# Splitting a V product stream between the sums of the next pair in a decode attention kernel

## The chip, the cores and the metric

The kernel runs on one core of a Trainium2 chip. The metric is device time in microseconds (us); before the change the median of three runs is 1988.61 us. A core has four engines that compute (TensorE for matmuls, VectorE, ScalarE, GpSimd), each with an instruction stream of its own, and SyncE, whose stream issues the large loads here. The streams meet only at semaphores. In the profile the engines are PE (and PEld for its weight loads), DVE, ACT, POOL and SP.

## The reference

Two independent attention blocks, A and B, each decode one token for two sequences, and their outputs are put side by side:

```python
def _A_ref(x, k_cache, v_cache, wq, wo):          # B = 2, Sq = 1, D = 640
    q = (x @ wq).reshape(B, Sq, Hq, Dh).transpose(0, 2, 1, 3)     # 32 heads of 192
    scores = jnp.einsum("bhqd,bhkd->bhqk", q, k) * (Dh ** -0.5)   # 8192 keys
    p = _softmax(scores, axis=-1)
    o = jnp.einsum("bhqk,bhkd->bhqd", p, v)
    return o.transpose(0, 2, 1, 3).reshape(B, Sq, Hq * Dh) @ wo
```

Everything is in bfloat16. Each block reads a K and a V cache of 2 x 32 x 8192 x 192 elements, each element once: 805 MB, and 837 MB with the weights.

## The kernel before

**Pairs.** The work is cut into 64 pairs (`NP`), each of two heads of one sequence. A pair's K is 6.3 MB, and so is its V. Both lie on 128 partitions: 64 partitions hold one head, and each holds 128 positions (`T`) of 192 elements.

**The ring of loads.** K and V go through three buffers of 6.3 MB (`ring`), in the order K0, V0, K1, V1 and so on; for the last two pairs it is K62, K63, V62, V63. SP issues them in that order (L134), each when its buffer is free: a K buffer when VectorE's fourth product of that K is done (`("m", i, 3)`), a V buffer when the last of its products on TensorE is done (`("pv", i)`). With three buffers, K of pair i+1 goes into the buffer of V of pair i-1, and V of pair i+1 into that of K of pair i. Since SP takes its stream in order, V's issue stands behind K's.

**A pair's scores.** The dot products of a one-row query are made in four quarters. VectorE multiplies a quarter of K by the query, which has been copied to all partitions (`add_mul`, L233; two product buffers `prod`). TensorE adds up the 192 elements in twelve steps of 16 with an identity matrix, into a PSUM tile of 32 x 16 (`add_sum`, L238; two tiles `scps`). VectorE reduces the last 16 (`add_red`, L245). The third product needs the buffer of sum 0, and the fourth that of sum 1. When four quarters are there, VectorE takes the maximum (`add_max`, L250 and L251), POOL takes it over the partitions (L254), and ScalarE makes exp in two halves with its sums (`add_exp`, L259 to L266), into `pb`.

**A pair's output.** `add_pv` has TensorE make one small matmul for the softmax sums (L274) and then 64 matmuls of `pb` with V (`T // 2`, L281), that add up in one PSUM tile (`ops`, two of them). Then ScalarE copies the odd head's part (`add_od`, L292), VectorE makes a reciprocal, an addition and a scaling (`add_on`, L296, L298, L300), and TensorE puts the result with four small matmuls in its place in a collecting tile (`add_place`, L310).

**The order.** Each engine's order is the order in which the main loop adds its operations to that engine's stream. For pair i TensorE runs: sum 0, sum 1, sum 2, the placing of pair i-1, the query of pair i+2 (L218), sum 3, the softmax sums and all 64 products of pair i. VectorE runs: products 0 and 1, the three small operations of pair i-1, reduction 0, product 2, reduction 1, product 3, reductions 2 and 3, the maximum. The last two pairs' products come after the loop, so that pair 63's sums run ahead of pair 62's products.

**Ahead and behind.** Before the loop the two query projections run from loads of 2 x 7.9 MB; behind it the output weights (2 x 7.9 MB, into the same ring) are multiplied with the collected outputs.

Of the kernel before, what the change touches and what calls it, by code (L numbers as in the profile page):

```python
# [51 lines left out]
def build_kernel(nc, blocks, out):  # L52
    NBLK = len(blocks)
    B, Hn, Sk, Dh = blocks[0]["k"].shape
# [4 lines left out]
    NP = NBLK * B * PB  # L59
    LAST = NP - 1  # L60
    T = 128
# [14 lines left out]
    def pair(i):  # L76
        blk, r = divmod(i, B * PB)
        b, ii = divmod(r, PB)
        return blk, b, ii

    with ExitStack() as es:
# [4 lines left out]
        ring = [sb(f"ring{i}", [128, RW], BF16) for i in range(3)]  # L86
# [4 lines left out]
        pb = [sb(f"pb{i}", [128, T // 2, 34], BF16) for i in range(2)]  # L91
# [18 lines left out]
        ops = [ps(f"ops{i}", [128, 512], F32) for i in range(2)]  # L110
# [6 lines left out]
        S_pe = _Stream("pe", sem("s_pe"), reg)  # L117
# [22 lines left out]
        slot_of = {}  # L140
# [6 lines left out]
        for blk in range(NBLK):  # L147
            w = blocks[blk]["wq"].rearrange("(j c) n -> j (c n)", c=DC)
# [23 lines left out]
        for blk, pieces in ((0, WA), (1, WB)):  # L172
            w = blocks[blk]["wo"].rearrange("(p r) n -> p (r n)", r=WR)
# [16 lines left out]
        def pr3(qd):  # L190
            return prod[qd % 2][:].rearrange("p (t d) -> p t d", d=Dh)

        def key(name, i, *rest):
            return (name, i) + rest if i >= 0 else None

        def before(i, qd, n):
            k = 4 * i + qd - n
            return (k // 4, k % 4) if k >= 0 else None
# [16 lines left out]
        def add_q(i):  # L215
            blk, b, ii = pair(i)
            r0 = 32 * blk
            S_pe.add(lambda eng: eng.matmul(qps[:, 0:2 * Dh], selb[r0:r0 + 2, b, :],  # L218
                                            qrow[r0:r0 + 2, 2 * ii * Dh:(2 * ii + 2) * Dh], start=True, stop=True),
                     waits=[("qe", blk, NQC - 1), ("init",), key("qt", i - 1)], sig=("q", i))  # L220

        def add_qt(i):
            def fn(eng):
                eng.activation(qt[i % 3][0:64, :], qps[0:64, 0:Dh], ACTF.Identity)  # L224
                return eng.activation(qt[i % 3][64:128, :], qps[64:128, Dh:2 * Dh], ACTF.Identity)  # L225
            S_act.add(fn, waits=[("q", i), key("m", i - 3, 3)], sig=("qt", i))

        def add_mul(i, qd):
            q = qt[i % 3][:].unsqueeze(1).broadcast_to([128, TQ, Dh])
            prev = before(i, qd, 2)  # L230
            w = [("k", i), ("qt", i)]
            w += [("s",) + prev] if prev else [("pr", 0, NQC - 1), ("pr", 1, NQC - 1)]
            S_dve.add(lambda eng: eng.tensor_tensor(pr3(qd), quarter(i, qd), q, ALU.mult), waits=w, sig=("m", i, qd))  # L233

        def add_sum(i, qd):
            def fn(eng):
                for j in range(NJ):
                    ins = eng.matmul(scps[qd % 2][:], ident[:], pr3(qd)[:, :, j * DG:(j + 1) * DG],  # L238
                                     start=(j == 0), stop=(j == NJ - 1))
                return ins  # L240
            prev = before(i, qd, 2)
            S_pe.add(fn, waits=[("m", i, qd), ("init",), ("r",) + prev if prev else None], sig=("s", i, qd))

        def add_red(i, qd):
            S_dve.add(lambda eng: eng.tensor_reduce(sc[i % 2][:, qd * TQ:(qd + 1) * TQ], scps[qd % 2][:], AXL.X, ALU.add),  # L245
                      waits=[("s", i, qd), key("exp", i - 2)], sig=("r", i, qd))

        def add_max(i):
            def fn(eng):
                eng.tensor_reduce(mp[i % 2][0:64, 0:1], sc[i % 2][0:64, :], AXL.X, ALU.max)  # L250
                return eng.tensor_reduce(mp[i % 2][64:128, 1:2], sc[i % 2][64:128, :], AXL.X, ALU.max)  # L251
            S_dve.add(fn, waits=[("r", i, 0), ("r", i, 1), ("r", i, 2), ("r", i, 3), key("ar", i - 2), ("init",)],
                      sig=("mx", i))
            S_pool.add(lambda eng: eng.partition_all_reduce(mg[i % 2][:], mp[i % 2][:], 128, bass.bass_isa.ReduceOp.max),  # L254
                       waits=[("mx", i), key("nb", i - 2)], sig=("ar", i))
# [14 lines left out]
                return ins  # L270
            S_act.add(fn, waits=[("nb", i), ("r", i, 3), key("pv", i - 2), key("l", i - 2), ("init",)], sig=("exp", i))

        def add_pv(i):
            S_pe.add(lambda eng: eng.matmul(ops[i % 2][0:2, 448:449], rs[i % 2][:], ones[:], start=True, stop=True),  # L274
                     waits=[("exp", i), key("on", i - 2), ("qe", 1, NQC - 1), ("init",)], sig=("l", i))
            vv = ring[slot_of["v", i]][:].rearrange("p (j f) -> p j f", f=2 * Dh)

            def part(j0, j1):
                def fn(eng):
                    for j in range(j0, j1):  # L280
                        ins = eng.matmul(ops[i % 2][0:34, 0:2 * Dh], pb[i % 2][:, j, :], vv[:, j, :],  # L281
                                         start=(j == 0), stop=(j == T // 2 - 1))
                    return ins
                return fn
            if i == LAST:
                S_pe.add(part(0, T // 4), waits=[("exp", i), ("v", i)])
                S_pe.add(part(T // 4, T // 2), waits=[("v2", i)], sig=("pv", i))
            else:
                S_pe.add(part(0, T // 2), waits=[("exp", i), ("v", i)], sig=("pv", i))

        def add_od(i):
            S_act.add(lambda eng: eng.activation(oodd[i % 2][:], ops[i % 2][32:34, Dh:2 * Dh], ACTF.Identity),  # L292
                      waits=[("pv", i), key("on", i - 2)], sig=("od", i))

        def add_on(i):
            S_dve.add(lambda eng: eng.reciprocal(rc[i % 2][:], ops[i % 2][0:2, 448:449]),  # L296
                      waits=[("l", i), ("pv", i), key("on", i - 2)], sig=("rc", i))
            S_dve.add(lambda eng: eng.tensor_tensor(oodd[i % 2][:], ops[i % 2][0:2, 0:Dh], oodd[i % 2][:], ALU.add),  # L298
                      waits=[("od", i)], sig=("ad", i))
            S_dve.add(lambda eng: eng.tensor_scalar(on[i % 2][:], oodd[i % 2][:], rc[i % 2][:], None, ALU.mult),  # L300
                      waits=[("rc", i), ("ad", i), key("pl", i - 2)], sig=("on", i))

        def add_place(i):
            blk, b, ii = pair(i)
            sec = (blk * B + b) * WR

            def fn(eng):
                for a in range(4):
                    at = 128 - (8 * ii + a)
                    ins = eng.matmul(oall[:, sec:sec + WR], place[:, at:at + 128], on[i % 2][:, a * WR:(a + 1) * WR],  # L310
                                     start=(ii == 0 and a == 0), stop=(ii == PB - 1 and a == 3))
                return ins
            w = [("on", i), ("init",)]
            if ii == 0 and i > 0:
                w.append(("oa", i // PB - 1))
            S_pe.add(fn, waits=w, sig=("pl", i))
            if ii == PB - 1:
                S_act.add(lambda eng: eng.activation(oallS[blk][:, :, b], oall[:, sec:sec + WR], ACTF.Identity),
                          waits=[("pl", i)], sig=("oa", i // PB))
# [43 lines left out]
        def fn_x(eng):  # L363
            for c in range(DC):
# [4 lines left out]
                  waits=[("xp",)], sig=("xT",))  # L369
        for blk in range(NBLK):  # L370
            for n in range(NQC):
                add_proj(blk, n)
            if blk == 0:
                for i in range(2):
                    add_q(i)
                    add_qt(i)

        for i in range(NP):
            tail = i >= NP - 2
            add_mul(i, 0)  # L380
            add_mul(i, 1)
            add_sum(i, 0)
            if i and i < LAST:
                add_od(i - 1)
                add_on(i - 1)
            add_red(i, 0)
            add_mul(i, 2)
            add_sum(i, 1)
            add_red(i, 1)
            add_mul(i, 3)  # L390
            add_sum(i, 2)
            if i and i < LAST:
                add_place(i - 1)
            add_red(i, 2)
            if i + 2 < NP:
                add_q(i + 2)
                add_qt(i + 2)
            add_sum(i, 3)
            add_red(i, 3)
            add_max(i)  # L400
            add_exp(i)
            if not tail:
                add_pv(i)
        for i in (NP - 2, NP - 1):
            add_pv(i)
            add_od(i)
            add_on(i)
            if i == NP - 2:
                add_place(i)
# [77 lines left out]
```

## Time and profile before

| what | us |
|---|---|
| median of three runs | 1988.61 (1987.79 to 1988.74) |
| profiled execution, its time | 1987.13 |
| profiled execution, its span | 1985.3 |
| VectorE's products, 256 of | 3.352 each, 852.7 in all |
| TensorE's products with V, 4096 of | 809.4 busy in all |
| TensorE's sums, 3072 matmuls | 700.1 busy in all |
| first product of VectorE starts | 56.67 |
| last K is issued | 1891.96 |

The span runs from the first instruction to the last of the slowest core, and is a little shorter than the time. A matmul's recorded length is longer than its distance to the next, since matmuls overlap; so a stream's length is read from the start of its first to the start of what follows. A group that is "idle before" an instruction names what ended the wait. Where a line of the timeline has an entry "x64", it merges that many instructions.

TensorE's clock is granted in stretches of 3.41 us; over the span it was 0.917 of full speed on average, alternating between full and half.

### The profile page before, as it was taken

To read this page: it belongs to the slowest core of one execution; us is meant where nothing else is said; L and a number is where in the kernel's file an instruction comes from. 1 tells how busy PE (TensorE), PEld (TensorE's weight loads), DVE (VectorE), ACT (ScalarE), POOL (GpSimd) and SP (SyncE) were. 2 spreads that over 40 slices of the span, in tenths; PEclk is the share of its full clock that TensorE was granted. 3 is DMA by queue.
4 is the path that set the end of the run, shared out by engine and by line. 5 is a ranking of instruction groups with operands and counts; after the bars stand their busy time and mean duration, and the time that the engine had idled before them with its cause. 6 is when DMAs were issued, how large, how long until landed. Compare 5 with 4: busy or idle time off the path is not lost.

```text
span 1985.3 us, 17767 instructions
## 1 busy us (share of the span) xinstructions
PE 1578.6 (80%) x7933; PEld 762.0 (38%) x7933; DVE 1095.1 (55%) x833; ACT 186.9 (9%) x610; POOL 32.2 (2%) x82
## 2 busy tenths in 40 slices
PE   4777877877877877877877877877877877878878
PEld 1333433433433433433433433433433433433434
DVE  0655655655555655655555565555555555565561
ACT  2111001011011011011011010010010010010000
POOL 1000000000000000000000000000000000000000
PEclk9989989989899989989889899889989889899889
DMA  9999999999999999999999999999999999999999
GB/s 412 437 428 430 439 427 427 426 424 415 413 430 429 410 431 410 432 427 421 416 424 426 419 425 418 420 429 418 421 418 426 421 424 419 423 424 420 415 428 380
DMA packets 20836, 837.91 MB, mean 422 GB/s; under 512 B 2316, under 2 KB 2584, under 8 KB 2968
## 3 DMA queue, kind: packets, MB, share of 16 engines
q1 hardware_dynamic: 20744, 836.78, 99.1%
q8 instruction: 62, 1.02, 0.2%
q14 instruction: 14, 0.11, 0.0%
q10 hardware_dynamic: 16, 0.01, 0.0%
HBM read 836.77 MB, written 0.01 MB: 421 GB/s over the span
## 4 chain that ended last, share of the span: by engine, by line
issue 91%; PE 4%; DMA 3%; DVE 2%; POOL 1%; SPq 0%; ACT 0%; POOLq 0%; DVEq 0%
DMA prod<-in_B_wq_dram 2%; PE ops L281 2%; DVE prod L233 1%; POOL mg L254 1%; PE scps L238 1%; PE ops L205 1%; DMA ring<-in_B_wo_dram 1%; DVE sc L245 0%; SPq L134 0%; ACT pb L266 0%; POOLq L43 0%; DVE mp L251 0%; ACT out_sb L333 0%; PE ops L274 0%; DVE oodd L298 0%
## 5 line engine op out<-in xcount | busy, mean ns | idle before, releaser
L233 DVE TENSOR_TENSOR prod<-ring,qt 128x6144 bf16<-128x6144 bf16 x256 | 852.7, 3352 | 388.2 <-DMA ring<-in_A_k_cache_dram 183.0
L238 PE MATMUL scps<-prod,ident 128*128 128x512 bf16 x3072 | 700.1, 381 | 152.6 <-DVE prod L233 152.6
L281 PE MATMUL ops<-ring,pb 128*34 128x384 bf16 x4096 | 809.4, 367 | 0.0
L281 PEld LDWEIGHTS ops<-ring,pb 128*34 128x34 bf16 x4096 | 440.3, 109 | 346.4 <-issue 138.2
L238 PEld LDWEIGHTS scps<-prod,ident 128*128 128x128 bf16 x3072 | 285.7, 98 | 538.7 <-DVE prod L233 198.9
L245 DVE TENSOR_REDUCE sc<-scps 128x32 f32<-128x512 f32 x256 | 176.1, 688 | 247.3 <-PE scps L238 247.3
L274 PE MATMUL ops<-ones,rs 128*2 128x1 f32 x128 | 12.2, 164 | 224.0 <-ACT pb L266 224.0
L296 DVE RECIPROCAL rc<-ops 2x1 f32<-2x1 f32 x64 | 10.0, 156 | 219.5 <-PE ops L281 219.5
L274 PEld LDWEIGHTS ops<-ones,rs 128*2 128x2 f32 x128 | 5.5, 82 | 255.1 <-ACT pb L266 254.6
L292 ACT ACTIVATE oodd<-ops 2x192 f32<-2x192 f32 x64 | 20.6, 321 | 820.3 <-PE ops L281 820.3
L266 ACT ACTIVATE pb<-sc,nb 64x128 bf16<-64x128 f32 x128 | 81.4, 636 | 3.1
L224 ACT ACTIVATE qt<-qps 64x192 bf16<-64x192 f32 x64 | 20.7, 323 | 566.7 <-PE qps L218 566.7
L254 POOL PARTITION_ALL_REDUCE mg<-mp x64 | 25.8, 404 | 1903.7 <-DVE mp L251 1903.7
L259 ACT ACTIVATE nb<-mg 64x1 f32<-64x1 f32 x64 | 13.0, 203 | 323.2 <-POOL mg L254 323.2
L266 ACT ACTIVATION_READ_ACCUMULATOR pb<-sc,nb 64x1 f32 x128 | 38.3, 299 | 0.0
L205 PE MATMUL ops<-ring,xT 128*2 128x512 bf16 x96 | 28.4, 425 | 12.4 <-DMA prod<-in_A_wq_dram 10.5
L298 DVE TENSOR_TENSOR oodd<-ops,oodd 2x192 f32<-2x192 f32 x64 | 22.1, 345 | 12.0 <-ACT oodd L292 12.0
L218 PE MATMUL qps<-qrow,selb 2*128 2x384 bf16 x64 | 20.8, 325 | 1.4 <-ACT qt L225 0.8
L310 PEld LDWEIGHTS oall<-on,place 2*128 2x128 bf16 x256 | 10.3, 92 | 28.1 <-issue 26.5
L300 DVE TENSOR_SCALAR on<-oodd,rc 2x192 bf16<-2x192 f32 x64 | 19.7, 307 | 2.3
L225 ACT ACTIVATE qt<-qps 64x192 bf16<-64x192 f32 x64 | 20.8, 325 | 0.8
L205 PEld LDWEIGHTS ops<-ring,xT 128*2 128x2 bf16 x96 | 8.7, 91 | 27.5 <-issue 17.6
(33 smaller groups left out, 131.0 us busy)
## 6 DMA issues: line engine op xcount, KB each, us to landing
ring<-in_A_k_cache_dram SPq DMA_DIRECT2D x32, 6144.0 KB, 20.4
ring<-in_A_v_cache_dram SPq DMA_DIRECT2D x32, 6144.0 KB, 24.7
ring<-in_B_k_cache_dram SPq DMA_DIRECT2D x32, 6144.0 KB, 19.6
ring<-in_B_v_cache_dram SPq DMA_DIRECT2D x31, 6144.0 KB, 23.6
ring<-in_A_wq_dram SPq DMA_DIRECT2D x1, 6144.0 KB, 17.5
ring<-in_B_wq_dram SPq DMA_DIRECT2D x1, 6144.0 KB, 35.3
ring<-in_B_v_cache_dram SPq DMA_DIRECT2D x2, 3072.0 KB, 20.2
ring<-in_A_wo_dram SPq DMA_DIRECT2D x2, 3040.0 KB, 14.7
```

What stands on the lines that cost most here:

```text
L205: ins = eng.matmul(ops[n % 2][32 * blk:32 * blk + 2, 0:QC], xT[:, c, 2 * blk:2 * blk + 2], src, start=(c == 0), stop=(c == DC - 1))
L218: S_pe.add(lambda eng: eng.matmul(qps[:, 0:2 * Dh], selb[r0:r0 + 2, b, :], qrow[r0:r0 + 2, 2 * ii * Dh:(2 * ii + 2) * Dh], start=True, sto ...
L224: eng.activation(qt[i % 3][0:64, :], qps[0:64, 0:Dh], ACTF.Identity)
L225: return eng.activation(qt[i % 3][64:128, :], qps[64:128, Dh:2 * Dh], ACTF.Identity)
L233: S_dve.add(lambda eng: eng.tensor_tensor(pr3(qd), quarter(i, qd), q, ALU.mult), waits=w, sig=("m", i, qd))
L238: ins = eng.matmul(scps[qd % 2][:], ident[:], pr3(qd)[:, :, j * DG:(j + 1) * DG], start=(j == 0), stop=(j == NJ - 1))
L245: S_dve.add(lambda eng: eng.tensor_reduce(sc[i % 2][:, qd * TQ:(qd + 1) * TQ], scps[qd % 2][:], AXL.X, ALU.add), waits=[("s", i, qd), key( ...
L254: S_pool.add(lambda eng: eng.partition_all_reduce(mg[i % 2][:], mp[i % 2][:], 128, bass.bass_isa.ReduceOp.max), waits=[("mx", i), key("nb" ...
L266: ins = eng.activation(pb[i % 2][p0:p0 + 64, :, h::32], sc[i % 2][p0:p0 + 64, :].rearrange("p (j a) -> p j a", a=2), ACTF.Exp, bias=nb[i % ...
L281: ins = eng.matmul(ops[i % 2][0:34, 0:2 * Dh], pb[i % 2][:, j, :], vv[:, j, :], start=(j == 0), stop=(j == T // 2 - 1))
L292: S_act.add(lambda eng: eng.activation(oodd[i % 2][:], ops[i % 2][32:34, Dh:2 * Dh], ACTF.Identity), waits=[("pv", i), key("on", i - 2)], ...
L298: S_dve.add(lambda eng: eng.tensor_tensor(oodd[i % 2][:], ops[i % 2][0:2, 0:Dh], oodd[i % 2][:], ALU.add), waits=[("od", i)], sig=("ad", i))
```

## The change

The softmax sums and the 64 products of `add_pv` become `add_l` and a product stream in parts. For pairs 0 to 61 the first 52 products stay directly behind exp; the next six come behind sum 0 of the next pair, and the last six behind sum 1. Only the last part signals `("pv", i)`. ScalarE's copy follows the last part in the program; VectorE's three small operations move from ahead of reduction 0 to behind reduction 2; the placing matmuls move from behind sum 2 to behind sum 3. The last two pairs keep their order.

```diff
-        def add_pv(i):
+        def pv_part(i, j0, j1):
+            vv = ring[slot_of["v", i]][:].rearrange("p (j f) -> p j f", f=2 * Dh)
+
+            def fn(eng):
+                for j in range(j0, j1):
+                    ins = eng.matmul(ops[i % 2][0:34, 0:2 * Dh], pb[i % 2][:, j, :], vv[:, j, :],
+                                     start=(j == 0), stop=(j == T // 2 - 1))
+                return ins
+            return fn
+
+        def add_l(i):
             S_pe.add(lambda eng: eng.matmul(ops[i % 2][0:2, 448:449], rs[i % 2][:], ones[:], start=True, stop=True),
                      waits=[("exp", i), key("on", i - 2), ("qe", 1, NQC - 1), ("init",)], sig=("l", i))
...
+        def add_pv(i, j0, j1):
+            w = [("exp", i), ("v", i)]
+            if i == LAST and j0:
+                w.append(("v2", i))
+            S_pe.add(pv_part(i, j0, j1), waits=w, sig=("pv", i) if j1 == T // 2 else None)
...
+        J = T // 2
+        J1, J2 = J - 12, J - 6
         for i in range(NP):
-            tail = i >= NP - 2
+            mid = 0 < i < LAST
             add_mul(i, 0)
             add_mul(i, 1)
             add_sum(i, 0)
-            if i and i < LAST:
-                add_od(i - 1)
-                add_on(i - 1)
+            if mid:
+                add_pv(i - 1, J1, J2)
             add_red(i, 0)
             add_mul(i, 2)
             add_sum(i, 1)
+            if mid:
+                add_pv(i - 1, J2, J)
+                add_od(i - 1)
             add_red(i, 1)
             add_mul(i, 3)
             add_sum(i, 2)
-            if i and i < LAST:
-                add_place(i - 1)
             add_red(i, 2)
+            if mid:
+                add_on(i - 1)
             if i + 2 < NP:
                 add_q(i + 2)
                 add_qt(i + 2)
             add_sum(i, 3)
+            if mid:
+                add_place(i - 1)
             add_red(i, 3)
             add_max(i)
             add_exp(i)
-            if not tail:
-                add_pv(i)
+            if i < NP - 2:
+                add_l(i)
+                add_pv(i, 0, J1)
```

More of the change, by code (lines that the diff above doesn't have):

```diff
@@ L271, in add_exp @@
             S_act.add(fn, waits=[("nb", i), ("r", i, 3), key("pv", i - 2), key("l", i - 2), ("init",)], sig=("exp", i))
-        def add_pv(i):
+        def pv_part(i, j0, j1):
[7 more added lines that the diff above has]
+        def add_l(i):
             S_pe.add(lambda eng: eng.matmul(ops[i % 2][0:2, 448:449], rs[i % 2][:], ones[:], start=True, stop=True),
                      waits=[("exp", i), key("on", i - 2), ("qe", 1, NQC - 1), ("init",)], sig=("l", i))
[L276 to L289, printed above, removed]
+        def add_pv(i, j0, j1):
[3 more added lines that the diff above has]
+            S_pe.add(pv_part(i, j0, j1), waits=w, sig=("pv", i) if j1 == T // 2 else None)
         def add_od(i):
@@ L401, in build_kernel @@
             add_exp(i)
-            if not tail:
-                add_pv(i)
+            if i < NP - 2:
+                add_l(i)
+                add_pv(i, 0, J1)
         for i in (NP - 2, NP - 1):
-            add_pv(i)
+            add_l(i)
+            if i == LAST:
+                add_pv(i, 0, J // 2)
+                add_pv(i, J // 2, J)
+            else:
+                add_pv(i, 0, J)
             add_od(i)
```

## The prediction

> **What bounds the kernel now.** The forecast is 2002 us, a little slower than the 1988.61 us of before.
>
> I began with the page: how busy the engines and the transfer queue are.
>
> ```profile
> PE 1578.6 (80%) x7933; PEld 762.0 (38%) x7933; DVE 1095.1 (55%) x833; ACT 186.9 (9%) x610; POOL 32.2 (2%) x82
> PEclk9989989989899989989889899889989889899889
> ...
> q1 hardware_dynamic: 20744, 836.78, 99.1%
> ```
>
> The loads' queue fills 99.1% of the 16 engines, so it looks like a kernel bound by transfers. Two windows of the same stream say that this is not all:
>
> ```profile
> 100.00:300.00 200.00, 161.49 (x796) 78.79 (x797) 111.26 (x86) 17.89 (x61) 2.48 (x7) 0.91 1.00 431
> 300.00:1850.00 1550.00, 1245.14 (x6173) 602.59 (x6172) 889.46 (x675) 137.69 (x470) 18.42 (x52) 0.91 1.00 422
> ```
>
> The last number is GB/s. With a full queue the loads go at 431; later at 422, though the busy share reads 1.00 in both. Something paces them. The page's chain of waits does not say what (91% of it is "issue"), so I read one pair in the timeline (start, duration):
>
> ```profile
> 942.64 0.19 PE L274 MATMUL ops<-ones,rs 128*2 128x1 f32 x2 [3.61 <-ACT pb L266]
> ...
> 942.76 12.26 PE L281 MATMUL ops<-ring,pb 128*34 128x384 bf16 x64
> ...
> 944.62 6.63 DVE L233 TENSOR_TENSOR prod<-ring,qt 128x6144 bf16<-128x6144 bf16 x2 [4.25 <-DMA ring<-in_A_k_cache_dram]
> ...
> 954.94 5.35 PE L238 MATMUL scps<-prod,ident 128*128 128x512 bf16 x24
> 955.04 0.33 SPq L134 DMA_DIRECT2D ring<-in_A_k_cache_dram  x1
> ...
> 957.75 0.69 DVE L245 TENSOR_REDUCE sc<-scps 128x32 f32<-128x512 f32 x1 [1.66 <-PE scps L238]
> 958.35 3.35 DVE L233 TENSOR_TENSOR prod<-ring,qt 128x6144 bf16<-128x6144 bf16 x1
> ...
> 962.22 3.35 DVE L233 TENSOR_TENSOR prod<-ring,qt 128x6144 bf16<-128x6144 bf16 x1
> ...
> 965.60 0.33 SPq L134 DMA_DIRECT2D ring<-in_A_v_cache_dram  x1
> ...
> 965.63 2.76 PE L238 MATMUL scps<-prod,ident 128*128 128x512 bf16 x12 [0.83 <-DVE prod L233]
> 968.43 0.69 DVE L245 TENSOR_REDUCE sc<-scps 128x32 f32<-128x512 f32 x1 [2.26 <-PE scps L238]
> ...
> 972.00 0.19 PE L274 MATMUL ops<-ones,rs 128*2 128x1 f32 x2 [3.61 <-ACT pb L266]
> ```
>
> The steps close into a ring without any transfer in it: exp's end to the end of the 64 products 12.30, sum 0 to its reduction 2.81, to the third product of VectorE 0.60, to the fourth 3.87, to sum 3 3.41, to reduction 3 2.80, from there through max, POOL and exp to the next pair 3.57: 29.36, the whole distance of 942.64 to 972.00. K landed at 944.62 and its first sum waited until 954.94 for the products. So the **order of work on TensorE** sets the pace. The issues of K loads at 89.42 and 1852.42 lie 59 pairs apart: 29.88 us each.
>
> The transfers are close behind. The trace's landing times (last of a load's 16 engines) give, with a full queue, 14.53 us from one load's landing to the next: 29.06 a pair, 0.82 under the ring. K of the next pair is issued when the previous V's products release its slot, and how early that is decides what its transfer costs. I set, for 61 pairs, the **lead** (landing of the V before it, less the issue) against the distance of the two landings:
>
> | lead, us | pairs | V's landing to K's landing, us |
> |---|---|---|
> | under 4 | 16 | 15.62 (14.53 to 17.18) |
> | 4 to 5 | 19 | 15.06 |
> | 5 to 6 | 14 | 14.59 |
> | over 6 | 12 | 14.55 |
>
> A short lead costs a load up to 2.7 us: the engines finish V some 2 to 4 us apart, and those that finish first stand empty or start slowly. V, issued 7 to 14 us ahead, costs 14.56 in the first seven pairs and 14.83 later. This table is the heart of the forecast.
>
> **The change, part by part.** *TensorE's ring.* A product takes 0.164 us at full clock ((89.32 - 78.81)/64). Twelve leave the stretch between exp and sum 0: 1.97 off the ring, 29.88 - 1.97 = 27.91. That is under the transfers' 29.06, so the ring no longer sets the pace, and a pair's work now hangs on its K landing. The held-back products fill gaps: six behind sum 0, six behind sum 1. Between sum 0's end and sum 2 (which waits for VectorE's third product) there are 0.11 + 0.60 + 3.35 us, 4.06 and some hundredths; sum 1 (2.70, from 1941.90 to the next matmul at 1944.60) and twelve products (1.97) are 4.67. Sum 2 is late by 0.6 at most, and reduction 2 waits for VectorE's fourth product anyway. Cost nothing; without this cover, 0.6 x 62 = 37 us.
>
> *VectorE's three small operations, ScalarE's copy and the placing matmuls.* Moved behind reduction 2, the three (0.16 + 0.35 + 0.31 with gaps: 1.05) lie inside sum 3, in which VectorE idled 2.26. The copy (0.32) now follows the second part on an engine 9% busy; the four placing matmuls (0.27) fall under max and exp, where TensorE idles 3.61. Nothing; uncovered, 1.05 x 62 = 65 us. POOL's order is untouched.
>
> *The release of V's slot, and the queue behind it.* This has a price. SP waits for the last product (its waits for them total 1196.8 us in 64 times) and then issues K; V's issue is queued behind. With K landing at 0: VectorE's first product ends at 3.38, sum 0 starts 0.06 later (3.44) and takes 2.70; six products 0.99 (7.13); sum 1, whose input is ready at 6.72, 2.70 (9.83); six products 0.99 (10.82); SP 0.10 after: **issue at 10.9**. Before, it was 10.16 on average from pair 11 on, and 8.16 in the first eleven. Four more changes of the stationary operand may add 0.1 each (gaps of 0.32 and 0.42 stand at such changes before), so 10.8 to 11.3. V's issue follows the fourth product of VectorE at 14.6, not at 21: its lead over K grows to about 15.
>
> Does sum 0 really start at 3.44? Reduction 0 then starts at 6.7, the fourth product ends at 14.5, sum 3 starts at 14.6, reduction 3 at 17.4, the sums of exp at 21.0. 52 products end at 29.6, plus 1.7 to 2.9 for the half-clock stretch (products took 10.57 in the pair at 78.81, 12.26 and 13.40 later): 31.3 to 32.5. At a period of 30.0 that is 1.3 to 2.5 into the next pair, before 3.44. So yes.
>
> *Sum.* V's lead being long, V takes 14.56. K's lead is 14.56 - 10.9 = 3.7, always, where before it swung between 2.3 and 9.8. The table's lowest row says 15.62, the next 15.06; the nine pairs whose issue came 10.5 to 11 after the K landing show 15.45, and I take that: 14.56 + 15.45 = 30.01 a pair. From K of pair 1 (landed 84.60) to K of pair 62 (1901.05) before needed 1816.45, 29.78 a pair; now 61 x 30.01 = 1830.6, +14.2. Head: as before. Tail: after K of pair 62 the next K comes with a full queue (15.29 before, -0.7), V of pair 62 pays the short lead (14.38 before, +1.0), and the output weights, issued 3.5 us ahead before, get a longer lead (-0.8): -0.5. Sum +13.7. The profiled execution took 1987.13 (span 1985.3), so 2000.8 for one like it; the median of the runs is 1.5 above it: **2002**. Bounds of K's distance, 14.9 (spread of the engines shrinks, since the early ones now wait every time) to 15.9 (issue at 11.3 and a wide spread): 29.46 to 30.46, -20 to +41 us: 1969 to 2030. The likeliest case's own range is 1993 to 2020.
>
> A row against my own value: at the issue of 418.83, made 0.3 us before the first engine ran empty, the first packets started 0.95 later, though packets that followed took about 2.5 us where 1.8 is usual. The Trainium skill, "DMA: Bandwidth & Descriptors" (Latency and other measured facts), has about 0.6 us from a hardware queue's issue to its first byte. By that rule a lead of 3.7 would hide the start for all engines, which is the far end of rival A; the table above speaks against it, with losses at leads up to 5.
>
> **The rivals.** *A, the shorter ring pays (25%).* If the engines' finishes draw together, K's lead is as good as 4 to 5 was: 14.56 + 15.06 = 29.62, -10 us; if it costs nothing, 29.1, -41 us. For it: pairs with leads of 3.17 and 3.48 cost 14.53 and 14.78. Against: the row's mean. Time about 1976 (1947 to 1984); 5 of the 25% are for the far end, a lead that hides all.
>
> *B, a wash (10%).* K's distance settles at 15.2: 29.8, within 4 us of 1989. Also what comes if the ring does not get shorter, because something in it that I hold for hidden is not.
>
> *C, the clock (13%), slower.* Place: the gap between the last of the 52 products and sum 0. In this trace, TensorE went to half clock after each 3.41 us window with under about 0.4 of matmul time (once 0.5), and returned after one of 0.8 or more. Now TensorE idles 0.9 to 2.1 us there; after a pair whose products met little or no half clock, over 3 (0.164 x 52 ends at 29.6). From some 2.1 us on, a window can fall under 0.4: sum 0 and what follows run at half clock, the issue comes 1.5 later, at 12.4. The pairs issued after 11 showed 15.48, and the one at 12.35 17.18; at 16.3 a pair is 30.9, +67 us, 2055. The Trainium skill, "TensorE: Matmul & The Clock Gate" (Part 1, the two states), gives an idle window of about 3.4 us for this; the trace agrees with windows of 3.41. By half of the pairs: 2028.
>
> **How the numbers follow.** Forecast 52%, A 25%, B 10%, C 13%. 0.2% (4 us) is about what a measurement tells from no change. Faster 25% (A), same 10% (B), slower 65% (forecast and C). The range 1968 to 2032 leaves out the lower part of A and most of C, about 2 in 10.
>
> **What would show it.** Right: products split 52, 6, 6; the K issue 10.8 to 11.3 after VectorE's first product starts; the wait for K before that product directly followed, 3.4 later, by sum 0; K's landing to K's landing near 30.0, without the fixed four-pair pattern of issues (29.37, 30.50, 30.61, 28.98). The first windows, 100 to 300, fall from 431 GB/s to about 420. Wrong if that window stays at 430 (A); if sum 0 starts later than 3.5 after the landing (then the ring still binds); or if half clock shows in sum 0 and 1 (C).

## The result

The changed kernel takes 2037.38 us (median of four runs, 2034.07 to 2045.21) against 1988.67 us before: a ratio of 1.0251, 95% interval 1.0222 to 1.0281. It is slower by 48.7 us. The forecast was 2002 us, with 1968 to 2032 as its range: the direction was right, the size was not. The profiled execution took 2037.92 us, with a span of 2036.1 (1985.3 before).

The same lines of the page as before, now of the changed kernel: engines, granted clock by slices, the loads' queue.

```profile
PE 1616.5 (79%) x7933; PEld 748.8 (37%) x7933; DVE 1081.5 (53%) x833; ACT 187.1 (9%) x610; POOL 32.2 (2%) x82
...
PEclk9998988888998988989888988988999999898989
...
q1 hardware_dynamic: 20744, 836.78, 97.1%
```

The queue of loads is less full (97.1% of the engines' time, 99.1% before), and the clock's slices no longer repeat. The two windows that were shown of before (length, busy times, clock, busy share of the transfers, GB/s):

```profile
100.00:300.00 200.00, 161.26 (x781) 75.54 (x778) 105.27 (x83) 17.56 (x60) 2.48 (x7) 0.91 0.98 414
300.00:1850.00 1550.00, 1245.10 (x6031) 577.62 (x6032) 858.64 (x663) 135.63 (x462) 18.07 (x51) 0.91 0.97 412
```

431 and 422 GB/s before are now 414 and 412, from the first pairs on. The page's chain of waits, which had been 91% "issue", now names transfers:

```profile
issue 62%; DMA 20%; PE 12%; DVE 5%; POOL 1%; SPq 0%; ACT 0%; POOLq 0%; DVEq 0%
```

The timeline of two neighbouring pairs (start, duration) shows what happens inside:

```profile
939.36 6.63 DVE L233 TENSOR_TENSOR prod<-ring,qt 128x6144 bf16<-128x6144 bf16 x2 [11.90 <-DMA ring<-in_A_k_cache_dram]
...
942.77 2.76 PE L238 MATMUL scps<-prod,ident 128*128 128x512 bf16 x12 [2.62 <-DVE prod L233]
...
945.47 1.15 PE L278 MATMUL ops<-ring,pb 128*34 128x384 bf16 x6
...
949.24 1.15 PE L278 MATMUL ops<-ring,pb 128*34 128x384 bf16 x6
...
950.42 0.33 SPq L134 DMA_DIRECT2D ring<-in_A_k_cache_dram  x1
...
960.27 8.62 PE L278 MATMUL ops<-ring,pb 128*34 128x384 bf16 x52
968.47 6.63 DVE L233 TENSOR_TENSOR prod<-ring,qt 128x6144 bf16<-128x6144 bf16 x2 [10.59 <-DMA ring<-in_A_k_cache_dram]
...
971.88 4.45 PE L238 MATMUL scps<-prod,ident 128*128 128x512 bf16 x12 [2.99 <-DVE prod L233]
...
976.26 1.15 PE L278 MATMUL ops<-ring,pb 128*34 128x384 bf16 x6
...
980.04 1.15 PE L278 MATMUL ops<-ring,pb 128*34 128x384 bf16 x6
...
981.22 0.33 SPq L134 DMA_DIRECT2D ring<-in_A_k_cache_dram  x1
```

VectorE waits longer for K (11.90 and 10.59; 4.25 and 4.27 before), and sum 0, which before stood behind the 64 products, now follows VectorE's first product directly, 3.41 after its start: the transfers set the pace. In the first pair K is issued 11.06 after VectorE's start. In the second it is 12.75, because sum 0 took 4.45 instead of 2.76: TensorE stood idle for 3.0 us ahead of it, after 52 products at full clock (8.62), and its clock had gone to half. The two sums in windows of their own (the third number from the end is the granted clock; the two behind it, of the transfers, say little over so short a stretch):

```profile
942.77:945.47 2.70, 2.70 (x12) 1.09 (x12) 0.00 (x0) 1.00 0.80 346
971.88:976.26 4.38, 4.38 (x12) 1.52 (x12) 0.00 (x0) 0.61 1.17 505
```

**Where the 48.7 us come from.** From the landings of K of pair 1 and K of pair 62 (84.57 and 1949.22) the 61 pairs between took 1864.65, 30.57 each, 48.2 more than before. By the clock of sum 0, the trace splits them (means, us; a "distance" is from the landing of the load before to its own landing):

| pairs | K issue after K landing | V's distance | lead over V | K's distance | sum |
|---|---|---|---|---|---|
| 35, sum 0 at full clock | 11.1 | 14.85 | 3.7 | 15.43 | 30.28 |
| 26, sum 0 at half clock | 13.0 | 14.60 | 1.6 | 16.36 | 30.96 |

Against the 29.78 of before, the first are 35 x 0.50 = 17 us, the second 26 x 1.18 = 31 us. The tail behind K of pair 62 took 2.6 us more. In total 50.8, which is the difference of the spans of the two profiled executions; the medians lie 48.7 apart.

### The profile page after: what moved, and what is told of

Its sections match the earlier page's. It is cut to its first block, busy times and chain, and to the rows that moved or that the text cites. A ratio compares the mean times of both kernels' runs of the same rounds, so it can differ in the third digit from the quotient of the medians.

```text
span 2036.1 us, 17767 instructions
## 1 busy us (share of the span) xinstructions
PE 1616.5 (79%) x7933; PEld 748.8 (37%) x7933; DVE 1081.5 (53%) x833; ACT 187.1 (9%) x610; POOL 32.2 (2%) x82
## 3 DMA queue, kind: packets, MB, share of 16 engines
q1 hardware_dynamic: 20744, 836.78, 97.1%
## 4 chain that ended last, share of the span: by engine, by line
issue 62%; DMA 20%; PE 12%; DVE 5%; POOL 1%; SPq 0%; ACT 0%; POOLq 0%; DVEq 0%
DMA ring<-in_B_k_cache_dram 17%; PE scps L238 7%; DVE prod L233 4%; PE ops L278 4%; DMA prod<-in_B_wq_dram 2%; DMA ring<-in_B_wo_dram 1%; PE ops L205 1%; POOL mg L254 1%; DVE sc L245 0%; SPq L134 0%; ACT pb L266 0%; POOLq L43 0%; DVE mp L251 0%; PE ops L284 0%; ACT out_sb L335 0%
## 5 line engine op out<-in xcount | busy, mean ns | idle before, releaser
L238 PE MATMUL scps<-prod,ident 128*128 128x512 bf16 x3072 | 762.5, 402 | 172.6 <-DVE prod L233 170.4
L278 PE MATMUL ops<-ring,pb 128*34 128x384 bf16 x4096 | 788.1, 354 | 0.0
L278 PEld LDWEIGHTS ops<-ring,pb 128*34 128x34 bf16 x4096 | 416.0, 105 | 359.9 <-issue 151.4
L238 PEld LDWEIGHTS scps<-prod,ident 128*128 128x128 bf16 x3072 | 292.1, 102 | 592.5 <-DVE prod L233 213.1
L312 PEld LDWEIGHTS oall<-on,place 2*128 2x128 bf16 x256 | 10.3, 92 | 28.1 <-issue 26.6
L327 PE MATMUL outps<-ring,oallS 128*2 128x320 bf16 x192 | 14.5, 299 | 7.0 <-DMA ring<-in_B_wo_dram 6.9
```

## Experiments

Each was run beside the kernel before on one chip. All are edits of the changed kernel, unless the text says before.

**The split taken back, the other moves kept.**

```diff
-                add_pv(i, 0, J1)
+                add_pv(i, 0, J)
...
-                add_pv(i - 1, J1, J2)
...
-                add_pv(i - 1, J2, J)
```

> The changed order with the split taken back: all 64 products directly behind exp again, while VectorE's three small operations stay behind reduction 2 and the placing matmuls behind sum 3. Theory (only the late release of V's slot and what follows from it costs): the ring of before is back, 29.9 us a pair, 1985 to 1993 us. Rival 1 (the moved small operations or placing matmuls are not hidden): about 2037 us stays. Rival 2 (they were a help that the split covered up): under 1980 us.

Measured: 1989.22 us, ratio 1.0000 (0.9991 to 1.0010). With all 64 products behind exp, the moved small operations and placing matmuls cost nothing and bring nothing; the loss comes with the split.

**The twelve products in one part behind sum 0.**

```diff
-        J1, J2 = J - 12, J - 6
+        J1 = J - 12
...
-                add_pv(i - 1, J1, J2)
+                add_pv(i - 1, J1, J)
+                add_od(i - 1)
...
-                add_pv(i - 1, J2, J)
-                add_od(i - 1)
```

> The changed order with the last twelve products in one part behind sum 0 instead of six behind sum 0 and six behind sum 1. Theory (release of V's slot): K is issued 3.44 + 2.70 + 1.97 + 0.1 = 8.2 us after the K landing at full clock, some 9.8 where sum 0 meets half clock; the lead over V's landing is 6.3 or 4.7, K's transfer takes 14.6 to 15.1, a pair 29.1 to 29.7: 1947 to 1984 us, faster than before. Rival 1 (half clock in the sums is the whole cost, the release costs nothing): sum 0 still meets half clock, about 2037 us. Rival 2 (leaving TensorE's stream between sums costs in itself): 2037 us or more.

Measured: 1954.75 us, ratio 0.9824 (0.9809 to 0.9838). The same number of products leaves the ring, but V's slot is released one sum earlier: K is issued 8.55 us after the K landing on average, with a lead of 6.09, and takes 14.61; a pair takes 29.25. The windows of this kernel, with the same columns as above:

```profile
100.00:300.00 200.00, 167.31 (x823) 80.55 (x824) 115.28 (x91) 17.91 (x61) 2.50 (x7) 0.91 1.00 432
300.00:1850.00 1550.00, 1277.78 (x6300) 613.51 (x6299) 897.36 (x689) 141.13 (x480) 18.89 (x53) 0.92 1.00 431
```

The full rate of the first pairs of before now holds to the end. So shortening TensorE's ring does pay, and taking twelve products out of the stream is not what loses it again. Sum 0 ran at half clock in 3 pairs here instead of 26, so this run alone does not part the release from the clock; the kernels with filled gaps below do. It is the first kernel that beats both.

**TensorE kept busy in both of its gaps.** A helper issues idle matmuls into a PSUM bank of its own:

```diff
+        def add_fill(n):
+            def fn(eng):
+                for _ in range(n):
+                    eng.matmul(warm[:], ident[:], ident[:].unsqueeze(1).broadcast_to([128, 4, 128]), start=True, stop=True)
+            S_pe.add(fn)
...
             if i < NP - 2:
+                add_fill(12)
                 add_l(i)
                 add_pv(i, 0, J1)
+                add_fill(12)
```

> The changed order with two groups of twelve idle matmuls on TensorE (identity by identity into a PSUM bank of their own, 2.6 us at full clock) in its two gaps, behind the placing matmuls and behind the 52 products; the computation is unchanged. Theory (release costs in every pair, half clock on top of it in 26 of 61): K is issued 11.1 us after the K landing in every pair, a pair takes 30.0 to 30.3 as the 34 undisturbed pairs did, 2002 to 2020 us. Rival 1 (the release alone, the clock costs nothing): 2037 us stays. Rival 2 (the clock alone): all is gone and the ring is shorter, 1950 us.

Measured: 2016.43 us, ratio 1.0129 (1.0107 to 1.0151). In the profiled execution sum 0 ran at half clock in 6 pairs instead of 26. The 54 pairs issued 10.6 to 11.5 us after the K landing (mean 11.09) had 15.45 for K, 14.69 for V, and 30.14 in all. So about 21 of the 49 us went with the half clock, and most of the rest stayed with the release at full clock.

**Before, with the gap under exp filled.**

```diff
             if not tail:
+                add_fill(12)
                 add_pv(i)
```

> The order of before with one group of twelve idle matmuls on TensorE in the gap that exp leaves (behind sum 3, ahead of the softmax sums); the computation is unchanged. Theory (before is bound by TensorE's ring, of which 1.7 to 2.9 us a pair are half clock): products stay at full clock, the ring is 27.7, transfers set the pace at 29.1 a pair with a full queue: 1945 to 1955 us. Rival 1 (before is bound by its transfers at 422 GB/s): 1988 us stays. Rival 2 (the idle matmuls are in the way of the softmax sums): over 1992 us.

Measured: 1954.56 us, ratio 0.9824 (0.9810 to 0.9839). In its timeline the idle matmuls end (982.52) before exp does (983.50), and the 64 products, with no half clock in them, take 10.58:

```profile
962.09 6.63 DVE L234 TENSOR_TENSOR prod<-ring,qt 128x6144 bf16<-128x6144 bf16 x2 [9.88 <-DMA ring<-in_A_k_cache_dram]
965.21 0.33 SPq L135 DMA_DIRECT2D ring<-in_B_k_cache_dram  x1
...
979.77 2.75 PE L295 MATMUL warm<-ident 128*128 128x512 bf16 x12
...
983.67 10.58 PE L282 MATMUL ops<-ring,pb 128*34 128x384 bf16 x64
```

K's issue comes 3.1 us after VectorE's start (the mean lead over V is 11.6), and a pair takes 29.24. That before was bound by TensorE's ring, with half clock inside it, is shown: matmuls that compute nothing made it 1.8% faster.

**The dose of the release**, in the kernel with both gaps filled: the parts changed from 52, 6, 6 to 58, 3, 3, and to 46, 9, 9.

```diff
-        J1, J2 = J - 12, J - 6
+        J1, J2 = J - 6, J - 3
```

> The filled kernel with parts of 58, 3 and 3 products instead of 52, 6 and 6; computation unchanged. Theory (a price set by the lead alone): the issue comes 6 x 0.164 = 1.0 us earlier, 10.1 us after the K landing, lead 4.5, K's distance about 15.0 by the row of 4 to 5, a pair 29.65: 34 us under the filled kernel, about 1982 us (1972 to 1995). Rival (breaking up the stream is what costs, not when it ends): as the filled kernel, 2016 us.

```diff
-        J1, J2 = J - 12, J - 6
+        J1, J2 = J - 18, J - 9
```

> The filled kernel with parts of 46, 9 and 9 products; computation unchanged. Theory (lead): the issue comes 1.0 us later than in the filled kernel, 12.1 us after the K landing, lead 2.5, K's distance about 16.2, a pair 30.8: 39 us over the filled kernel, about 2055 us (2040 to 2075). Rival (breaking up the stream costs, not when it ends): 2016 us. Rival 2 (a shorter ring pays as well): under 2016 us.

Measured: 1989.13 us (0.9999, 0.9990 to 1.0009) and 2051.22 us (1.0309, 1.0277 to 1.0340). With the filled 52, 6, 6 between them at 2016.43, the time follows the release: means of the issue after the K landing 10.31, 11.27 and 12.57; K's distance 15.14, 15.54 and 16.07; pairs 29.80, 30.21 and 30.93. In the first, 12 of 60 pairs were issued at 10.6 or later, where the theory had 10.1: 58 products and twelve idle matmuls held sum 0 up in 27 pairs, by up to 0.65. In the second, sum 0 met half clock in 18 pairs, in spite of the filling. The pairs whose sum 0 was on time and at full clock give the dose by itself: with the issue at 10.11 (31 pairs), 11.09 (53) and 12.06 (42), K's distance was 14.91, 15.43 and 15.77.

**Parts of 52 and 12, both gaps filled.**

> Parts of 52 and 12 with both gaps of TensorE filled; computation unchanged. Theory (transfers are the floor once K's lead is over 6 us): half clock or not no longer matters, 29.2 us a pair, 1950 to 1957 us as without the filling. Rival (half clock still costs there): 1945 us or less.

Measured: 1956.89 us (0.9833, 0.9818 to 0.9847), 29.27 a pair. Once K's lead is 6 us, the clock no longer matters: the granted clock was 0.997 here and 0.920 without the filling, and the time is no better. Against the filled 52, 6, 6, which takes 2016.43 with as many products held back and a granted clock of 0.990, the earlier release is worth some 60 us.

**Only the gap ahead of sum 0 filled**, with ten idle matmuls:

```diff
                 add_pv(i, 0, J1)
+                add_fill(10)
```

> The changed order with ten idle matmuls (2.2 us at full clock) behind the 52 products alone; the gap under exp is left, so the products still meet half clock. Theory (half clock costs where it falls into sum 0, because that moves the issue; in the 52 products it is hidden): as with both gaps filled, 2005 to 2022 us, a few us more where products at half clock and the idle matmuls together end behind sum 0's start. Rival (half clock in the products costs too): 2030 us or more.

Measured: 2045.49 us (1.0291, 1.0265 to 1.0316). The expectation missed, and the number is the rival's. Sum 0 never ran at half clock here, but in half of the pairs it came late. One of them:

```profile
935.45 11.28 PE L279 MATMUL ops<-ring,pb 128*34 128x384 bf16 x52
...
944.90 6.63 DVE L234 TENSOR_TENSOR prod<-ring,qt 128x6144 bf16<-128x6144 bf16 x2 [11.85 <-DMA ring<-in_A_k_cache_dram]
...
946.66 2.33 PE L297 MATMUL warm<-ident 128*128 128x512 bf16 x10
...
948.83 2.75 PE L239 MATMUL scps<-prod,ident 128*128 128x512 bf16 x12
```

The products took 11.28 with half clock in them, the idle matmuls came behind, and VectorE's first product (3.35) had been done for 0.6 us when sum 0 could start, 3.93 after that product's start instead of 3.41. In 29 of 60 pairs sum 0 started over 3.5 us after the start of VectorE's first product, in the mean of these 4.5 and at most 5.8. The run therefore doesn't separate the two theories; the next one was made for that.

**Only the gap under exp filled.**

```diff
             if i < NP - 2:
+                add_fill(12)
                 add_l(i)
                 add_pv(i, 0, J1)
```

> The changed order with twelve idle matmuls in the gap under exp alone, so that the 52 products run at full clock and end early, and TensorE's gap ahead of sum 0 is at its widest; computation unchanged. Theory (half clock costs only where it falls into sum 0, and a wide gap ahead of sum 0 brings it there): sum 0 meets half clock in nearly all pairs instead of 26 of 61; with some 31.0 us a pair instead of 30.6 the time grows to 2050 to 2070 us, though the granted clock in the products is better. Rival (more time at full clock is a help wherever it falls): 2037 us or less.

Measured: 2074.24 us (1.0423, 1.0406 to 1.0440), 4 us above the expected range and the slowest of all, though the granted clock is higher than in the changed kernel (0.938 to 0.916). Sum 0 met half clock in 50 of 60 pairs. One of them:

```profile
975.48 8.62 PE L279 MATMUL ops<-ring,pb 128*34 128x384 bf16 x52
...
985.31 6.63 DVE L234 TENSOR_TENSOR prod<-ring,qt 128x6144 bf16<-128x6144 bf16 x2 [12.23 <-DMA ring<-in_A_k_cache_dram]
...
988.73 5.20 PE L239 MATMUL scps<-prod,ident 128*128 128x512 bf16 x12 [4.63 <-DVE prod L234]
...
998.81 0.33 SPq L135 DMA_DIRECT2D ring<-in_A_k_cache_dram  x1
```

The products are at full clock and done at 984.1, TensorE is idle for 4.63, sum 0 takes 5.20, and K is issued 13.5 after VectorE's start. Full clock in the products is worth nothing there; it widens the gap and moves the half clock into the stretch that ends with the issue.

## Why the prediction was right and wrong

**Right: what bounds before.** The ring on TensorE, with half clock in it, and transfers just behind: before with its gap filled goes to 29.24 a pair, where the forecast put the transfers' floor at 29.06.

**Right: what the moves cost.** The small operations, the copy and the placing matmuls were put at nothing; the run with the split taken back is within 0.1%.

**Right: the price of the late release, and the table of leads.** At full clock the issue was forecast 10.9 after the K landing and came at 11.1; K's distance was forecast at 15.45 and was 15.43 in the changed kernel's 35 undisturbed pairs, 15.45 in the filled kernel. These are means: single pairs of the 35 lay between 14.50 and 16.97. The rows also hold beyond the kernel they were read from: leads of 3 to 4 us cost 15.54 (27 pairs) and of 4 to 5 14.90 (6 pairs) after the change; only the five pairs with 4 to 5 in the filled kernel stand out, at 15.70. Rival A's condition came true without its gain: a V's 16 landings drew together, to 2.16 us from first to last on average (2.85 before), and K cost no less at the same lead. Why a lead of 3.7 us does not cover a spread of some 2 us, no run took apart. The Trainium skill, "DMA: Bandwidth & Descriptors" (Latency and other measured facts), has about 0.6 us from a hardware queue's issue to its first byte. By these rows that is not the measure of a sufficient lead; here 5 us and more were needed.

**Wrong: "So yes".** The step that asked whether sum 0 really starts 3.44 after the K landing answered only for its start. It started there in all but 3 of 60 pairs, but in 26 it ran at half clock. The forecast had charged every pair 1.7 to 2.9 us of half clock in the products, and so had them end late and the gap ahead of sum 0 be short. That held while the pairs kept step with the clock's stretches of 3.413 us, as before (35 stretches are the 119.46 us in which its pattern of four pairs repeats). At a mean period of 30.6 they don't keep step: the distance from one K issue to the next now changes between 28.1 and 33.3.

In 15 of 60 pairs the products met no half clock, and sum 0 behind them ran at half clock in all 15. In 30 pairs they lost about what the forecast had charged at the least (one stretch), and sum 0 still ran at half clock in 11: in these, K landed 31.07 after the K before it, in the other 19 30.23, so that a later K widened the gap. Behind the 15 with more half clock in the products it never did. The gap decides (counted from 0.164 us after the last product's start):

| idle ahead of sum 0 in the changed kernel, us | pairs | of them at half clock |
|---|---|---|
| under 2 | 23 | 0 |
| 2 to 3 | 14 | 5 |
| 3 and more | 23 | 21 |

This was rival C, with its place and nearly its price: 12.4 was forecast for the issue and 13.0 measured, 30.9 for such a pair and 30.96 measured, and its half way case, 2028, lies nearest of all cases to the result. That the price fits so well is in part luck: the issue came 0.6 later than C had it, and C's 16.3 for K's distance was chosen between a row of 15.48 and a single pair of 17.18. The mistake was to hold it as an alternative with a chance of 13%, when it is a term that comes on top of the forecast in a share of the pairs. C and the forecast happened together: 23 us of the 37 that the span's sum was short come from K's distance (15.83 on average for 15.45, times 61).

In this trace the stretches of 3.41 us at full clock that were followed by half clock had matmuls in at most 0.46 of their time, and those followed by full clock in at least 0.42; so a gap of 2 us can do, if it falls into one stretch (1.41 of 3.41 is 0.41). The Trainium skill, "TensorE: Matmul & The Clock Gate" (Part 1, the two states), has one idle window of about 3.4 us for this step down. The stretches of 3.413 us here agree with that length, but they did not have to be idle throughout: 5 of the 14 gaps of 2 to 3 us were followed by half clock too.

**Mis-sized: V.** V's distance was put at 14.56, from the first seven pairs of before, since its lead would be long. The row beside it, 14.83 for the later pairs with leads of 7 us and more, spoke against that and was passed over. V's lead was 15 us, and it took 14.74 on average: 11 us of the 37. Where K has a long lead as well, V took 14.58 (before, filled) and 14.64 (parts of 52 and 12). So V's excess does not come from its own lead. In the changed kernel V took 15.15 behind a K whose 16 landings lay within 1.5 us (13 pairs), and 14.53 where they lay over 2.5 us apart (18 pairs); so it goes with the state in which the K ahead left the engines, but no run took that apart.

**Mis-sized: the tail.** Forecast at -0.5, measured +2.6. V of pair 62, issued only 2.1 ahead after a last sum 0 at half clock, took 15.26, near what was charged. The K before it, put at 0.7 less than before for a full queue, took 15.98 (15.29 before), though it was issued 16.0 ahead; and what follows V of pair 62 took 1.1 longer instead of 0.8 less.

## What to carry to other kernels

When a buffer's last reader is moved later, price the load that waits for the buffer: read from the trace how the landings spread out as the lead over the load before shrinks, for the lead that is needed can be several times the start-up time (5 us here, against first packets 0.95 us after an issue). When a change makes an engine wait that did not wait before, ask where its clock's half-speed stretch will fall now, and charge it as a share of the iterations and not as another story. And look first at what the engine's idle gap costs: a few matmuls that compute nothing, or the same twelve products released in one part, gave 1.8% where the split in two parts lost 2.5%.

## What was not expected of the hardware

Matmuls without a purpose made a kernel faster (1989.66 to 1954.56 us), and in another place made one slower (2037 to 2074 us) at a higher granted clock. In before with its gap filled, where the queue was always full, the 16 engines drifted until a load's landings lay 8 to 10 us apart from first to last (2.55 at the first K), and still a load landed 14.62 us after the one ahead of it on average (14.53 in the median): the spread cost 0.1 us a load at most, with a mean lead over V of 11.6 us.
